# Rows of an expert stream sorted in fours, two blocks to a scatter, sixteen last slots

## The chip, the cores and the metric

The kernel runs on one core of a Trainium2 chip. Its time is device microseconds from launch to end, and lower is better. The kernel before takes 719.75 us (median of three runs, 718.98 to 726.15); the profiled execution has a span of 721.2 us and took 722.9 us.

Engines are named as in the profile: PE multiplies (PEld is its weight load), DVE works on vectors, ACT evaluates activations and copies, POOL here issues the indirect DMAs and zeroes a small tile, and SP issues the other DMAs. An indirect DMA is a scatter whose row addresses come from a tile.

## The reference

Eight sequences of 3584 tokens of 192 numbers go through a causal convolution of seven taps. Its taps are a softmax, one for each of eight groups of 24 channels. Then each of the 28,672 tokens goes to one of eight experts.

```python
logits = x @ w_gate                        # 28672 x 8, x is the convolution's result
e_idx = np.argmax(logits, axis=1)          # the token's expert
gate_w = probs[np.arange(N), e_idx]        # softmax of the logits
eom = 1.0 / (1.0 + np.exp(-(x @ w_output_gate)))
for e in range(E):
    mask = e_idx == e
    h = np.maximum(x[mask] @ w1[e], 0.0)   # 192 -> 1024
    ye = h @ w2[e]                         # 1024 -> 192
    out[mask] = gate_w[mask, None] * eom[mask, e, None] * ye
```

The inputs are drawn with a fixed seed. With them the experts get 3088, 3403, 4201, 3741, 3725, 3377, 3722 and 3415 tokens.

## The kernel before, in words

**Front.** The tokens come in 16 units of 1792. `front_a` (lines 356 to 424) convolves a unit with banded matrices (L367), transposes it (L390), multiplies it with the gates (L401) and transposes the logits back (L416). `front_b` (lines 427 to 550) picks each token's expert, counts, and sorts. A unit is sorted in eight steps of 224 tokens. In a step DVE makes two one-hot matrices `pm` of 120 x 256 (`prep`, L508) and gated rows `xrow` (L503). PE multiplies them in four products of 120 x 128 by 194 columns (L541). ACT copies the result into a tile `xs` (L548). The sorted rows of a step come as pairs: one partition of `xs` holds two rows of the same expert, so an expert's odd last row leaves a hole. One scatter (L559) writes the 128 partitions of `xs` to the DRAM stream `xcg`, where each expert has its own stretch. All counts and places (`R`, `DN`, `TP`, `CP`) are in pairs.

**Experts.** A slot is up to 512 rows of one expert's stretch. `slot_load` brings it in with two transposing DMAs, `xa` and `xb` (L682, L684), and the rows' token numbers `xi` (L686), all from SP. `Slot.first` multiplies with w1 (L727 with 128 rows of contraction, L734 with 64 rows, two at a time), and ACT and DVE apply the relu (L755, L753). `Slot.second` multiplies with w2 (L777). ACT copies 128 x 384 results to `y` (L783). Four scatters of 128 rows (L588) write a full slot's results to the output.

**Order.** The order is written out by hand. Before the main loop, units 0 to 3 are convolved and sorted. The main loop has iterations `u` = 2 to 13 of four slots each, and `u` = 14 with the last slots. A slot has four positions, so an iteration of four slots has positions 0 to 15. At each even position stands a `first` of half a slot, at each position a quarter of the `second` of the slot before. Around them the loop puts pieces of the front of later units. At positions 0 to 7 stand the eight sort steps of unit `u` + 2, one each, with the scatter of each right behind (`emit_in`). (In iteration 2 it is positions 3 to 10.) After position 7 SP gets the loads of the next iteration's slots. Output scatters are taken from a list by `quota`: one at each odd position among 0 to 7, then one and two in turn. `rest` puts a small POOL memset (L571) behind every second indirect DMA.

**Last slots.** `plan` chooses four experts for each iteration from 2 to 13 and takes up to 512 rows of each. For iteration 14, when all tokens are counted, it takes up to 512 rows of each of seven experts. Then `pick` chooses the expert with the most rows left, once for each entry of `DYN`: two slots of 512 rows and four of 256. For each, SP copies the expert's weights, 768 KB, to a tile `wd` (L704). What is still left goes through a loop at the end (L948), whose count is read from the rows left.

Of the kernel before, what the change touches and what calls it, by code (L numbers as in the profile page):

```python
# [11 lines left out]
FP16 = mybir.dt.float16  # L12
# [9 lines left out]
def kernel(  # L22
# [30 lines left out]
    TP = TT // 2  # L53
    NG = NB // 2
    CP = TP + N // 2 + 64
    CAP = 2 * CP
# [8 lines left out]
    DYN = (TP, TP) + (TP // 2,) * 4  # L65
# [5 lines left out]
    xcg2 = xcg.rearrange("(a b) w -> a (b w)", b=2)  # L71
# [153 lines left out]
    hole = const.tile([128, 1], FP32)  # L225
    nc.vector.tensor_scalar(out=rowi[:, 3:4], in0=rowi[:, 0:1], scalar1=63, scalar2=None,
                            op0=ALU.bitwise_and)
    nc.vector.tensor_copy(out=hole, in_=rowi[:, 3:4])
    nc.vector.tensor_scalar(out=hole, in0=hole, scalar1=float(HB), scalar2=-64.0,
# [22 lines left out]
    NXS = 12  # L252
    xss = [const.tile([128, 2, RW], FP16, name=f"xs{i}") for i in range(NXS)]
# [3 lines left out]
    poi = const.tile([128, 2, 128], U32)  # L257
    nc.gpsimd.iota(poi, pattern=[[1, 2], [2, 128]], base=1, channel_multiplier=0)
# [31 lines left out]
    for l in range(2):  # L290
        nc.vector.tensor_scalar(
            out=lsum[0:GE, l * GE:(l + 1) * GE].rearrange("p (i e) -> p i e", e=E),
            in0=s9[:, :, 0:E], scalar1=2.0, scalar2=None, op0=ALU.mult)
# [133 lines left out]
    def front_b(u, split=False):  # L427
# [30 lines left out]
        nc.vector.tensor_scalar(out=nu, in0=pn[:, 0:1], scalar1=1.0, scalar2=None,  # L458
                                op0=ALU.add)
        nc.vector.tensor_scalar(out=nu, in0=nu, scalar1=1, scalar2=None,  # L460
# [52 lines left out]
        if split:  # L513
# [10 lines left out]
            scalar=rowf[:, 0:1], in1=dd, op0=ALU.is_le, op1=ALU.mult)  # L524
        dst = pr.tile([128, NG], FP32, tag="dst", name="dst")
        nc.vector.tensor_reduce(out=dst, in_=dd, axis=AX.X, op=ALU.max)
        du = pr.tile([128, NG], U32, tag="du", name="du")
        nc.vector.tensor_scalar(out=du, in0=dst, scalar1=rowf[:, 0:1], scalar2=None, op0=ALU.add)
        prep(1)
        yield  # L530
        for i in range(NG):
            if i == 1 and u >= U0 and u != U0 + 2:
                v = u if u < U0 + 2 else u - 1
                plans[v] = plan(v)
            if i + 2 < NG:
                prep(i + 2)
# [7 lines left out]
            while len(pend) >= NXS:  # L544
                emit_in()
            xs = xss[nxs[0] % NXS]
            nxs[0] += 1
# [10 lines left out]
    def scatter(u, du, xs, i):  # L558
        i = nc.gpsimd.indirect_dma_start(  # L559
            out=xcg2, out_offset=bass.IndirectOffsetOnAxis(ap=du[:, i:i + 1], axis=0),  # L560
            in_=xs.rearrange("p r w -> p (r w)"), in_offset=None,
            bounds_check=E * CP - 1, oob_is_err=False)
        nodep(i, f"sc{u}", [f"sc{v}" for v in range(NU)] + ["load", "guard"])
# [40 lines left out]
    def plan_run(e0, n, nm):  # L604
# [8 lines left out]
        nc.vector.tensor_scalar(out=bu[:, 0:n], in0=bs, scalar1=2.0, scalar2=None, op0=ALU.mult)  # L613
        nc.vector.tensor_tensor(out=Dh, in0=Dh, in1=tk, op=ALU.add)
        nc.vector.tensor_scalar(out=tk, in0=tk, scalar1=-2.0, scalar2=float(TT),
# [15 lines left out]
    def plan(u):  # L631
        n = 4 if u < UL else E - 1
        e0 = nexte[0]
        nexte[0] = (e0 + n) % E
        p = plan_run(e0, min(n, E - e0), "a")
        if e0 + n > E:
            p += plan_run(0, e0 + n - E, "b")
        return p

    def pick(tp):  # L640
# [17 lines left out]
        nc.vector.scalar_tensor_tensor(out=bt, in0=bt, scalar=2.0, in1=oh,  # L658
# [9 lines left out]
        nc.vector.tensor_scalar(out=tk1, in0=tk1, scalar1=-2.0, scalar2=float(2 * tp),  # L668
# [39 lines left out]
    class Slot:  # L708
# [49 lines left out]
        def second(self, q):  # L758
# [15 lines left out]
            o = (q % 2) * D  # L774
            for fc in range(FCH):
                w = WA + (fc // 2 + fc % 2 * (FCH // 2)) * D
                nc.tensor.matmul(self.pp[:, o:o + D],  # L777
                                 self.ht[fc // 2][:, fc % 2, q * 128:(q + 1) * 128],
                                 self.w[:, w:w + D],
                                 start=(fc == 0 and q % 2 == 0),  # L780
                                 stop=(fc == FCH - 1 and q % 2 == 1))
            if q % 2 == 1:
                nc.scalar.copy(out=self.y[:, q - 1:q + 1, :],  # L783
                               in_=self.pp[:, 0:2 * D].rearrange("p (g d) -> p g d", d=D))
                pout.extend((self.y, self.oi, j) for j in (q - 1, q))
# [47 lines left out]
    def load_pick(tp):  # L833
        sel, bap, inv = pick(tp)
        base = reg(bap[0:1, 0:1], [ET.SP], E * CAP - TT)
        return w_dyn(sel), inv, slot_load(base, NU - 1, 2 * tp)
# [26 lines left out]
    for u in range(U0, UL + 1):  # L863
# [27 lines left out]
        while k < len(todo):  # L891
            w, inv, xabi = todo[k]
            s = Slot(xabi, w, inv)
            for q in range(4):
# [18 lines left out]
                if pos in sorting:  # L913
                    drain(fs, 1)
                    emit_in(len(pend))
# [22 lines left out]
    nc.vector.tensor_scalar(out=lfu, in0=lfu, scalar1=8, scalar2=None,  # L938
# [49 lines left out]
```

## Time and profile before

| | |
|---|---|
| time, median of 3 runs | 719.75 us |
| profiled execution, span | 722.9 us, 721.2 us |
| PE busy | 577.4 us (80%) |
| POOL busy | 419.3 us (58%) |
| DVE, ACT busy | 375.7 us, 364.8 us |
| stream scatters (L559) | 128, 128.9 us of POOL |
| output scatters (L588) | 236, 232.6 us of POOL |
| sort products (L541) | 512, 68.9 us of PE |
| first slot's first product, last iteration's first product | 100.3 us, 628.4 us |

So there are three stretches: the fill to 100.3 us, twelve iterations to 628.4 us (44.0 us each), and the last 13 slots to 721.2 us. The last two numbers of the table are the starts of L727 and L734 on the first and on the 49th slot. Read busy time by stretch, since the limits differ. The chain of waits follows the work that ended last back from the end. In it "another core or an unknown queue" is time in which the profile names no releaser; on one core this is no other core.

### The profile page before, as it was taken

How to read it: one execution, taken by the hardware profiler on the slowest of the kernel's cores; microseconds unless marked ns; L12 is line 12 of the kernel's file. 1: busy time of each engine (PE TensorE's matmuls, PEld its weight loads, DVE VectorE, ACT ScalarE, POOL GpSimd, SP SyncE). 2: the span in 40 equal slices, each digit the busy share in tenths (PEclk: the TensorE clock that was granted, in tenths of full speed). 3: DMA queues.
4: the chain of work that ended last, by engine and by line, in shares of the span. 5: the costliest groups of instructions: out<-in, count | busy, mean ns of one | idle time of the engine just before them, and what ended most of it. 6: DMA issues, size and time to landing. Idle time of an engine off the chain costs nothing.

```text
span 721.2 us, 16231 instructions
## 1 busy us (share of the span) xinstructions
PE 577.4 (80%) x5712; PEld 370.8 (51%) x5712; DVE 375.7 (52%) x1355; ACT 364.8 (51%) x657; POOL 419.3 (58%) x621
## 2 busy tenths in 40 slices
PE   8878868998497979869697897978969767688874
PEld 4545535664364646546364563644646434445552
DVE  6765547575344736546372673735638343146422
ACT  5765535664354635546363563644646444355552
POOL 8464443888455574655647355564655747555664
PEclk9976668999598998989899798997989989799998
DMA  9999493897555545355453544536142332576411
GB/s 166 235 265 225 105 190 78 165 197 149 112 126 115 126 118 129 93 131 129 108 126 109 102 124 103 135 100 130 69 101 71 88 80 74 118 161 199 156 55 36
DMA packets 161091, 91.95 MB, mean 127 GB/s; under 512 B 112373, under 2 KB 151910, under 8 KB 161008
## 3 DMA queue, kind: packets, MB, share of 16 engines
q1 hardware_dynamic: 131504, 47.57, 31.8%
q0 software_dynamic: 29504, 43.32, 22.7%
q8 instruction: 45, 0.74, 0.4%
q14 instruction: 38, 0.31, 0.2%
HBM read 37.87 MB, written 42.07 MB: 111 GB/s over the span
## 4 chain that ended last, share of the span: by engine, by line
PE 61%; another core or an unknown queue 10%; ACT 9%; issue 8%; DVE 5%; DMA 2%; POOL 2%; SPq 2%; POOLq 0%; ACTq 0%; DVEq 0%
PE pyt L777 18%; PE pp L727 16%; PE pp L734 8%; PE pf L541 6%; PE pf L367 6%; ACT ht L755 4%; PE pf L390 3%; PE pf L401 2%; DMA xt<-in_x_dram 1%; POOL out_dram L588 1%; ACT cv L349 1%; ACT tt L349 1%; ACT y L783 1%; DVE ht L753 1%
## 5 line engine op out<-in xcount | busy, mean ns | idle before, releaser
L588 POOL DMA_INDIRECT out_dram<-y,oi x236 | 232.6, 986 | 146.7 <-ACT y L783 82.3
L777 PE MATMUL pyt<-wres,ht 128*128 128x192 f16 x1760 | 188.3, 256 | 38.2 <-ACT y L783 20.9
L777 PEld LDWEIGHTS <-ht 128*128 128x128 f16 x1888 | 168.6, 101 | 82.6 <-issue 58.4
L559 POOL DMA_INDIRECT xcg_sorted<-xs,du x128 | 128.9, 1007 | 140.7 <-ACT xs L349 101.6
L755 ACT ACTIVATE ht<-pp 128x1024 f16<-128x1024 f32 (+1 forms) x183 | 176.5, 998 | 60.2 <-PE pp L727 30.1
L753 DVE TENSOR_SCALAR ht<-pp 128x1024 f16<-128x1024 f32 (+1 forms) x61 | 72.4, 1187 | 129.4 <-PE pp L727 92.4
L734 PE MATMUL pp<-xb,wres 64*128 64x512 f16 x220 | 75.6, 401 | 37.9 <-ACT ht L755 25.6
L783 ACT COPY y<-pyt 128x384 f32<-128x384 f32 x118 | 57.2, 484 | 94.6 <-remote 32.9
L727 PE MATMUL pp<-xa,wres 128*128 128x512 f16 x220 | 89.9, 409 | 1.3 <-issue 0.7
L727 PE MATMUL pp<-xb,wres 128*128 128x512 f16 x220 | 89.0, 404 | 2.2 <-issue 2.2
L367 PE MATMUL pf<-xt,band 64*64 64x192 f32 x1024 | 69.6, 368 | 20.9 <-issue 11.9
L349 ACT CAST xs<-pf 128x388 f16<-128x388 f32 x128 | 62.4, 496 | 43.1 <-PE pf L541 27.1
L734 PE MATMUL pp<-xa,wres 64*128 64x512 f16 x220 | 76.3, 404 | 1.3 <-issue 0.8
L541 PE MATMUL pf<-xrow,pm 120*128 120x194 f16 x512 | 68.9, 261 | 8.0 <-DVE pm L508 4.2
L351 DVE COPY cv<-pf 120x384 f32<-120x384 f32 x44 | 24.4, 556 | 96.5 <-remote 58.1
L727 PEld LDWEIGHTS <-wres 128*128 128x128 f16 x440 | 35.2, 101 | 64.1 <-issue 42.4
L349 ACT COPY cv<-pf 120x384 f32<-120x384 f32 x84 | 38.2, 486 | 55.1 <-remote 31.2
L508 DVE TENSOR_SCALAR pm<-pos,pos 120x256 f16<-120x256 f16 x256 | 61.5, 304 | 0.0
L503 DVE TENSOR_TENSOR xrow<-cv,gs 120x384 f16<-120x384 f32 x120 | 61.4, 550 | 0.0
L734 PEld LDWEIGHTS <-wres 64*128 64x128 f16 x440 | 18.4, 95 | 82.8 <-issue 82.1
L367 PEld LDWEIGHTS pf<-xt,band 64*64 64x64 f32 x1024 | 40.8, 146 | 36.9 <-issue 21.3
L541 PEld LDWEIGHTS <-pm 120*128 120x128 f16 x512 | 46.2, 102 | 16.9 <-DVE pm L508 6.5
(154 smaller groups left out, 526.0 us busy)
## 6 DMA issues: line engine op xcount, KB each, us to landing
xt<-in_x_dram SPq DMA_DIRECT2D x56, 384.0 KB
wd<-wres SPq DMA_DIRECT2D x6, 768.0 KB
out_dram<-y,oi POOLq DMA_INDIRECT x236
wres<-in_moe_w_dram POOLq DMA_DIRECT2D x8, 384.0 KB
xt<-in_x_dram SPq DMA_DIRECT2D x8, 336.0 KB
wres<-in_moe_w_dram POOLq DMA_DIRECT2D x8, 256.0 KB
xcg_sorted<-xs,du POOLq DMA_INDIRECT x128
xcg_sorted<-zrow SPq DMA_DIRECT2D x8, 256.0 KB
```

What stands on the lines that cost most here:

```text
L349: nc.scalar.copy(out=o, in_=i)
L367: nc.tensor.matmul(pcs[g][64 * c:64 * c + 64, o:o + NB // 2 * GH], band[64 * g:64 * g + 64, h + hh, :], xt[64 * g:64 * g + 64, c * NB // 2 ...
L508: nc.vector.tensor_scalar(out=pms[i][P, l, :], in0=pos16[P], scalar1=pos[P, l * NG + i:l * NG + i + 1], scalar2=None, op0=ALU.is_equal)
L541: nc.tensor.matmul(ps[:, r * XW:(r + 1) * XW], pm[P, l, r * 128:(r + 1) * 128], xr[P, l * NG + i, :], start=(r == 0 and l == 0), stop=(r = ...
L559: i = nc.gpsimd.indirect_dma_start(out=xcg2, out_offset=bass.IndirectOffsetOnAxis(ap=du[:, i:i + 1], axis=0), in_=xs.rearrange("p r w -> p ...
L588: i = nc.gpsimd.indirect_dma_start(out=out, out_offset=bass.IndirectOffsetOnAxis(ap=oi[:, j:j + 1], axis=0), in_=y[:, j, :], in_offset=Non ...
L727: nc.tensor.matmul(pps[r][:, l, :], w[:, o2:o2 + 128], x, start=(r == lead), stop=(r != lead))
L734: nc.tensor.matmul(pps[r][:, l, :], w[p0:p0 + 64, c:c + 128], x[p0:p0 + 64], start=(r != lead), stop=(r == lead))
L753: nc.vector.tensor_relu(out=ht, in_=pps[r])
L755: nc.scalar.activation(out=ht, in_=pps[r], func=AF.Relu)
L777: nc.tensor.matmul(self.pp[:, o:o + D], self.ht[fc // 2][:, fc % 2, q * 128:(q + 1) * 128], self.w[:, w:w + D], start=(fc == 0 and q % 2 = ...
L783: nc.scalar.copy(out=self.y[:, q - 1:q + 1, :], in_=self.pp[:, 0:2 * D].rearrange("p (g d) -> p g d", d=D))
```

## The change

A partition of `xs` now holds four rows of one expert (`QR` = 4), and all counts and places are in fours. A step's 224 tokens fill at most 64 such partitions, so two steps share one `xs` of 128 partitions and one scatter of 2 KB rows: four scatters a unit in place of eight. A step's one-hot matrix has the same 256 columns, read as four rows of 64. The products are 120 x 64 by 194 columns, and those of the two steps of a pair go side by side to columns 0 to 63 and 64 to 127 of PE. There are sixteen products for a pair of steps in place of eight. In the main loop both steps of a pair now stand at an odd position. The last iteration plans all eight experts, and `DYN` has eight entries: four slots of 512 rows, one of 256 and three of 128. Counted from the reference's routing, holes raise the stream's rows from 29,196 to 30,200, and with either kernel's last slots no row is left for the loop at the end.

```diff
-    TP = TT // 2
+    QR = 4
+    TP = TT // QR
...
-    CP = TP + N // 2 + 64
-    CAP = 2 * CP
+    NT = NG // 2
+    CP = TP + N // QR + 96
+    CAP = QR * CP
...
-    DYN = (TP, TP) + (TP // 2,) * 4
+    DYN = (TP,) * 4 + (TP // 2,) + (TP // 4,) * 3
...
-    NXS = 12
-    xss = [const.tile([128, 2, RW], FP16, name=f"xs{i}") for i in range(NXS)]
+    NXS = 6
+    xss = [const.tile([128, QR, RW], FP16, name=f"xs{i}") for i in range(NXS)]
...
-        du = pr.tile([128, NG], U32, tag="du", name="du")
-        nc.vector.tensor_scalar(out=du, in0=dst, scalar1=rowf[:, 0:1], scalar2=None, op0=ALU.add)
+        du = pr.tile([128, NT], U32, tag="du", name="du")
+        for g in range(2):
+            h = slice(64 * g, 64 * g + 64)
+            nc.vector.tensor_scalar(out=du[h], in0=dst[h].rearrange("p (t g) -> p g t", g=2)[:, g, :],
+                                    scalar1=rowm[h], scalar2=None, op0=ALU.add)
...
         for i in range(NG):
+            t, rh = i // 2, i % 2 * 2
...
-            pm = pms.pop(i)
             ps = pft()
             for r in range(2):
                 for l in range(2):
-                    nc.tensor.matmul(ps[:, r * XW:(r + 1) * XW],
-                                     pm[P, l, r * 128:(r + 1) * 128], xr[P, l * NG + i, :],
-                                     start=(r == 0 and l == 0), stop=(r == 1 and l == 1))
...
-            evac(xs[:, :, 0:XW], ps[:, 0:2 * XW].rearrange("p (r w) -> p r w", r=2), "act")
-            pend.append(lambda i=i, xs=xs: scatter(u, du, xs, i))
+                    for g in range(2):
+                        nc.tensor.matmul(
+                            ps[64 * g:64 * g + 64, r * XW:(r + 1) * XW],
+                            pms[2 * t + g][P, l, (rh + r) * 64:(rh + r + 1) * 64],
+                            xr[P, l * NG + 2 * t + g, :],
+                            start=(r == 0 and l == 0), stop=(r == 1 and l == 1),
+                            tile_position=(0, 64 * g))
...
+            evac(xs[:, rh:rh + 2, 0:XW], ps[:, 0:2 * XW].rearrange("p (r w) -> p r w", r=2), "act")
+            if rh:
+                pend.append(lambda t=t, xs=xs: scatter(u, du, xs, t))
...
-        n = 4 if u < UL else E - 1
+        n = 4 if u < UL else E
...
-                if pos in sorting:
-                    drain(fs, 1)
+                if pos in sorting and pos % 2:
+                    drain(fs, 2)
                     emit_in(len(pend))
```

PE, in the main loop, the end of a sort step before (`ht` is a slot's relu result, `pm` the one-hot matrix, `pf` the result in PSUM):

```order
L541 MATMUL pf_5411<-xrow1_249,pm_5320 128x194
L541 LDWEIGHTS pm_5320
L541 MATMUL pf_5411<-xrow1_249,pm_5320 128x194
L401 MATMUL pf_5423<-tt_5150,wg_128 32x224 x12
L734 LDWEIGHTS wres_307
```

and the middle of a pair of steps now, where the second half's result (`pf_5400`) begins:

```order
L549 LDWEIGHTS pm_5234
L549 MATMUL pf_5374<-xrow1_251,pm_5234 64x194
L549 LDWEIGHTS pm_5287
L549 MATMUL pf_5374<-xrow1_251,pm_5287 64x194
L549 LDWEIGHTS pm_5234
L549 MATMUL pf_5400<-xrow1_251,pm_5234 64x194
L549 LDWEIGHTS pm_5287
L549 MATMUL pf_5400<-xrow1_251,pm_5287 64x194
```

One step's `pm` fed four products in a row; now the `pm` of two steps alternate, product by product, through sixteen products.

POOL, in the main loop, from the sixth stream scatter of a unit to the outputs behind the last one, before:

```order
L559 DMA xcg_sorted<-xs_259,du 117248x512
L571 MEMSET idle 128x16
L559 DMA xcg_sorted<-xs_260,du 117248x512
L588 DMA out_dram<-y,oi 28672x192
L571 MEMSET idle 128x16
L559 DMA xcg_sorted<-xs_261,du 117248x512
L588 DMA out_dram<-y,oi 28672x192
L571 MEMSET idle 128x16
L588 DMA out_dram<-y,oi 28672x192 x2
```

and the last two stream scatters of a unit now:

```order
L572 DMA xcg_sorted<-xs_258,du 59136x1024
L601 DMA out_dram<-y,oi 28672x192
L584 MEMSET idle 128x16
L572 DMA xcg_sorted<-xs_259,du 59136x1024
L601 DMA out_dram<-y,oi 28672x192
L584 MEMSET idle 128x16
L601 DMA out_dram<-y,oi 28672x192 x2
```

Between two outputs there were one or two stream scatters and now there is one. Behind the last stream scatter of a unit stood twelve outputs up to the next unit's first; they stand there still, with a thirteenth, since the next unit's first stream scatter comes one position later.

## Rows read from the trace of the kernel before

**Rows 1.** The page: span, then busy time of each engine.
```profile
span 721.2 us, 16231 instructions
PE 577.4 (80%) x5712; PEld 370.8 (51%) x5712; DVE 375.7 (52%) x1355; ACT 364.8 (51%) x657; POOL 419.3 (58%) x621
```

**Rows 2.** Windows: stretch, length, busy time (count) of PE, PEld, DVE, ACT, POOL; clock.
```profile
367.20:387.60 20.40, 18.97 (x221) 13.57 (x222) 13.16 (x48) 12.53 (x22) 11.54 (x18) 1.00 0.48 122
387.60:413.10 25.50, 18.47 (x156) 10.73 (x153) 9.83 (x34) 9.90 (x17) 13.64 (x20) 0.80 0.48 104
628.40:690.60 62.20, 53.08 (x434) 31.89 (x433) 29.36 (x127) 34.21 (x45) 37.18 (x55) 1.00 0.58 159
690.60:721.20 30.60, 16.13 (x163) 11.25 (x160) 6.32 (x27) 9.80 (x19) 15.63 (x23) 0.91 0.13 44
```

**Rows 3.** Windows of line L727 alone (eight products a slot): PE busy (count), PEld.
```profile
100.30:628.40 528.10, 110.11 (x385) 31.17 (x386) 0.90 0.50 115
628.40:690.60 62.20, 21.58 (x72) 5.28 (x73) 1.00 0.58 159
```

**Rows 4.** Chain of waits, 374 to 386 us: start, length, what, count.
```profile
374.29 0.66 PE pyt L777 x8
374.95 0.34 PE pf L541 x4
...
381.38 1.72 PE pf L401 x24
...
385.27 0.22 PE pf L416 x2
```

**Rows 5.** Costliest groups: line, engine, names, shapes, count, busy us, mean ns, idle before.
```profile
L541 PE MATMUL pf<-xrow,pm 120*128 120x194 f16 x512 | 68.9, 261 | 8.0 <-DVE pm L508 4.2 <-issue 1.9 <-DVE xrow L503 1.4
L541 PEld LDWEIGHTS <-pm 120*128 120x128 f16 x512 | 46.2, 102 | 16.9 <-DVE pm L508 6.5 <-issue 6.4 <-DVE xrow L503 1.7
L367 PE MATMUL pf<-xt,band 64*64 64x192 f32 x1024 | 69.6, 368 | 20.9 <-issue 11.9 <-ACT cv L349 4.8 <-DVE gb L420 1.8
L559 POOL DMA_INDIRECT xcg_sorted<-xs,du x128 | 128.9, 1007 | 140.7 <-ACT xs L349 101.6 <-ACT tt L349 16.2 <-issue 15.9
L588 POOL DMA_INDIRECT out_dram<-y,oi x236 | 232.6, 986 | 146.7 <-ACT y L783 82.3 <-issue 45.7 <-DVE dd L522 4.9
```

**Rows 6.** POOL in order of time, 259 to 270 us: start, length, instruction, idle before.
```profile
259.59 0.97 POOL L559 DMA_INDIRECT xcg_sorted<-xs,du  x1 [1.75 <-ACT xs L349]
260.87 0.98 POOL L588 DMA_INDIRECT out_dram<-y,oi  x1 [0.30 <-issue]
...
268.58 0.99 POOL L588 DMA_INDIRECT out_dram<-y,oi  x1 [0.30 <-issue]
```

**Rows 7.** PE in order of time, 264 to 272 us.
```profile
264.25 0.87 PE L367 MATMUL pf<-xt,band 64*64 64x192 f32 x13
265.54 0.34 PE L367 MATMUL pf<-xt,band 64*64 64x192 f32 x1 [0.42 <-issue]
266.98 0.48 PE L367 MATMUL pf<-xt,band 64*64 64x192 f32 x2 [1.09 <-issue]
268.39 0.58 PE L734 MATMUL pp<-xb,wres 64*128 64x512 f16 x1 [0.94 <-issue]
...
271.26 0.60 PE L734 MATMUL pp<-xa,wres 64*128 64x512 f16 x1
```

**Rows 8.** The chain of waits, whole: shares by line, then two of its pieces.
```profile
by line: PE pyt L777 18.2%; PE pp L727 16.2%; another core or an unknown queue 10.4%; PE pp L734 8.5%; issue 7.9%; PE pf L541 5.7%; PE pf L367 5.7%; ACT ht L755 3.8%; PE pf L390 3.0%; PE pf L401 2.3%; DMA xt<-in_x_dram 1.2%; POOL out_dram L
...
94.19 4.05 another core or an unknown queue x2
...
388.83 7.99 another core or an unknown queue
```

**Rows 9.** POOL in order of time, 92 to 97 us, in the fill.
```profile
91.95 0.98 POOL L559 DMA_INDIRECT xcg_sorted<-xs,du  x1 [1.20 <-ACT xs L349]
...
95.80 0.98 POOL L559 DMA_INDIRECT xcg_sorted<-xs,du  x1 [0.31 <-issue]
```

More of the change, by code (lines that the diff above doesn't have):

```diff
@@ L225 @@
     hole = const.tile([128, 1], FP32)
+    rowm = const.tile([128, 1], FP32)
     nc.vector.tensor_scalar(out=rowi[:, 3:4], in0=rowi[:, 0:1], scalar1=63, scalar2=None,
@@ L228 @@
     nc.vector.tensor_copy(out=hole, in_=rowi[:, 3:4])
+    nc.vector.tensor_copy(out=rowm, in_=rowi[:, 3:4])
     nc.vector.tensor_scalar(out=hole, in0=hole, scalar1=float(HB), scalar2=-64.0,
@@ L251 @@
     nc.gpsimd.memset(lt, 0.0)
-    NXS = 12
-    xss = [const.tile([128, 2, RW], FP16, name=f"xs{i}") for i in range(NXS)]
+    NXS = 6
+    xss = [const.tile([128, QR, RW], FP16, name=f"xs{i}") for i in range(NXS)]
     for t in xss:
         nc.gpsimd.memset(t[:, :, XW:RW], 0.0)
-    poi = const.tile([128, 2, 128], U32)
-    nc.gpsimd.iota(poi, pattern=[[1, 2], [2, 128]], base=1, channel_multiplier=0)
+    poi = const.tile([128, QR, 64], U32)
+    nc.gpsimd.iota(poi, pattern=[[1, QR], [QR, 64]], base=1, channel_multiplier=0)
     pos16 = const.tile([128, 256], FP16)
@@ L457, in front_b @@
         nu = pr.tile([128, 1], U32, tag="nu", name="nu")
-        nc.vector.tensor_scalar(out=nu, in0=pn[:, 0:1], scalar1=1.0, scalar2=None,
+        nc.vector.tensor_scalar(out=nu, in0=pn[:, 0:1], scalar1=float(QR - 1), scalar2=None,
                                 op0=ALU.add)
-        nc.vector.tensor_scalar(out=nu, in0=nu, scalar1=1, scalar2=None,
+        nc.vector.tensor_scalar(out=nu, in0=nu, scalar1=2, scalar2=None,
                                 op0=ALU.logical_shift_right)
@@ L559, in scatter @@
         i = nc.gpsimd.indirect_dma_start(
-            out=xcg2, out_offset=bass.IndirectOffsetOnAxis(ap=du[:, i:i + 1], axis=0),
+            out=xcg4, out_offset=bass.IndirectOffsetOnAxis(ap=du[:, i:i + 1], axis=0),
             in_=xs.rearrange("p r w -> p (r w)"), in_offset=None,
@@ L657, in pick @@
                                        op0=ALU.add, op1=ALU.min)
-        nc.vector.scalar_tensor_tensor(out=bt, in0=bt, scalar=2.0, in1=oh,
+        nc.vector.scalar_tensor_tensor(out=bt, in0=bt, scalar=float(QR), in1=oh,
                                        op0=ALU.mult, op1=ALU.mult)
@@ L667, in pick @@
                                        op0=ALU.mult, op1=ALU.add)
-        nc.vector.tensor_scalar(out=tk1, in0=tk1, scalar1=-2.0, scalar2=float(2 * tp),
+        nc.vector.tensor_scalar(out=tk1, in0=tk1, scalar1=-float(QR), scalar2=float(QR * tp),
                                 op0=ALU.mult, op1=ALU.add)
@@ L774, in second @@
             o = (q % 2) * D
+            last = q % 2 == 1 or q == self.nq - 1
             for fc in range(FCH):
@@ L780, in second @@
                                  start=(fc == 0 and q % 2 == 0),
[L781 to L785, printed above, removed]
+                                 stop=(fc == FCH - 1 and last))
+            if last:
+                j0 = q - q % 2
+                nc.scalar.copy(out=self.y[:, j0:q + 1, :],
+                               in_=self.pp[:, 0:(q + 1 - j0) * D].rearrange("p (g d) -> p g d", d=D))
+                pout.extend((self.y, self.oi, j) for j in range(j0, q + 1))
     def reg(ap, engines, hi):
@@ L835, in load_pick @@
         base = reg(bap[0:1, 0:1], [ET.SP], E * CAP - TT)
-        return w_dyn(sel), inv, slot_load(base, NU - 1, 2 * tp)
+        return w_dyn(sel), inv, slot_load(base, NU - 1, QR * tp)
     xts[U0 + 3] = load_x(U0 + 3)
@@ L937 @@
     nc.vector.tensor_copy(out=lfu, in_=lf)
-    nc.vector.tensor_scalar(out=lfu, in0=lfu, scalar1=8, scalar2=None,
+    nc.vector.tensor_scalar(out=lfu, in0=lfu, scalar1=7, scalar2=None,
                             op0=ALU.logical_shift_right)
```

19 lines of the change are left out of this document (10 added, 9 removed).

## The prediction

> **What bounds the kernel now.** I read the busy times first. PE is busy 80% of the span and POOL 58%, so the scatters that the change halves are not on the engine with the most work [rows 1]. An average over the run hides the stretches, so I cut the main loop and the last slots into windows. In the first half of an iteration (367.2 to 387.6 us, with the sort steps) PE is busy 18.97 of 20.40 us. In the second half (387.6 to 413.1) it is busy 18.47 of 25.50: 7.0 us are lost there [rows 2]. The last slots are PE's as well: 53.08 of 62.20 us [rows 2].
>
> Where do the 7 us go? The chain of waits has 10.4% of the span, 75 us, without a releaser, in pieces like the 7.99 us at 388.83 [rows 8]. I looked at one of these with POOL beside PE. POOL waits for ACT's last `xs`, issues the last stream scatter at 259.59, and then seven output scatters without a pause until 269.57 [rows 6]. PE starts 13 products within 0.87 us at 264.25. From 265.54 on it starts one about every 1.4 us (265.54, 266.98, 268.39) and is still slow at 271.26 [rows 7]. So about 5 us into a run of back-to-back indirect DMAs PE slows, and it recovers 1 to 2 us after the run's end. The trace doesn't say why. It says that a long run costs PE time.
>
> **The change, part by part.** *Stream scatters.* 64 in place of 128 go, each 1.007 us of POOL [rows 5], and nine output scatters of 0.986 us come (245 in place of 236: 60 full slots of four, one half of two, three quarters of one). POOL gets 64.4 - 8.9 = 55.6 us less busy time. Most of this is worth nothing, since POOL idles 140.7 us ahead of these scatters, 101.6 of them for ACT's `xs` [rows 5]. If a scatter of 2 KB rows costs POOL twice as much, POOL is where it was, and no more.
>
> *Runs of scatters.* What could be worth something are the stalls of PE. The run that hurts begins with the last stream scatter of a unit, which waits for the last sort step in either kernel, and the seven outputs behind it were held back by `quota`, which is unchanged. In the order above the twelve outputs behind the last stream scatter stay as well. So this run keeps its eight scatters. Only where an earlier stream scatter was late too and joined the run does it become shorter. I take a tenth of the 75 us: **-7 us**. The bounds are 0 and the two scatters of 1.28 us (start to start in rows 6) that would leave each of twelve runs, -31 us.
>
> *Fill.* At 91.95 to 96.78 us four stream scatters run back to back [rows 9], and the chain has 4.05 us without a releaser at 94.19 [rows 8]. They become two. I take this piece as gone, **-4 us**. The bounds are 0 and -8, for a second such place. The rest of the fill keeps its convolutions and copies.
>
> *Sort products.* Four products now take 0.34 us [rows 4], so a pair of steps 0.68 us. In their place come 16 products of half the columns. Side by side without loss they take 0.68 us again. The nearest row is L401: 24 products of 224 columns in four column groups take 1.72 us on the chain, entry and exit included. L416 gives the rate of the same four-byte kind alone, 0.22 us for 2 x 128 columns or 0.86 ns a column [rows 4]. One after the other L401 would take 24 x 224 x 0.86 = 4.6 us, four at a time 1.16. So column groups do run side by side here, with 0.56 us of loss for 24 products, 0.37 for 16. L367, in groups of rows and columns, has 69.6 us for 64 blocks of 16 [rows 5], 1.09 each against 0.66. I take 0.25 us a pair, less than these two, as the loads are two-byte ones and the groups two. In the main loop there are 48 pairs, in the half of the iteration where PE has 1.4 us to spare, so all of it counts: **+12 us**. The 16 pairs in the fill I cost at nothing: PE waits there for other things, and without that cover they add 4 us. The lower bound is 0. The upper bound is a load of 0.102 us [rows 5] ahead of every product with nothing beside it: 16 x 0.102 = 1.63 us, 0.95 more a pair, +46 us. The Trainium skill, TensorEngine Tiling (Array Packing), under Restrictions and Gotchas, says that column tiling excludes the fast weight load, and under Key Properties that changing the tiling mode drains the engine. By that rule the sum would tend to this upper bound; the 1.72 us of L401 speak against it, as they hold loads and a change of mode too.
>
> *What moves with them.* A scatter leaves one step later for even steps and at the same step for the last, so the loads that SP holds until the last scatter of a unit has landed start when they did. ACT copies the same 128 results, two behind each other. They wait behind `y` now, which no longer stands between two of them. One more DVE instruction a unit writes `du`. Both engines are about 60% busy there (13.16 and 12.53 of 20.40 us) [rows 2]: nothing, and if `xs` came late, the next transposes would wait for a PSUM tile, a few tenths a pair, within the bound above.
>
> *Last slots.* The holes raise the stream from 29,196 to 30,200 rows. The slots' room grows from 59 x 512 to 61.25 x 512 rows, and slots are computed in full, however few rows they hold. 72 products of L727 at eight a slot are nine full slots in 62.20 us [rows 2, 3], 6.91 us each. Now there are twelve (eight planned, four picked): +20.7 us. Behind them stand one half and three quarter slots in place of four halves. The 30.60 us of these and the end hold 16.13 us of PE [rows 2], some 4 a slot. A quarter has half of a half's columns and results, at most 2 us less; I take 1.7, three times: -5.1. Sum **+15.6 us**. The bounds: +20.7 if a quarter costs what a half did, since its weights' copy is as large. Below, three full slots at PE's own 53.08 / 9 = 5.90 us, and the quarters at half of 30.60 / 4: 17.7 - 11.5 = +6.2. Two more copies of 768 KB run eight slots ahead of their use, and the DMA engines are 58% busy there (the last but one number in rows 2).
>
> The sum is 15.6 + 12 - 7 - 4 = **+16.6 us**. It is made against the profiled execution (722.9 us, 721.2 of them span: 739.5). That one lies 3.2 us above the median of the runs shown, so I add the difference to the median: 719.75 + 16.6 = **736 us**. The likeliest case has 727 to 752 as its own range.
>
> **Rivals.** *The runs get shorter (faster).* If PE is slowed not by the run alone but by all the indirect DMAs of the 10 us before it, half the stream scatters take two off each run: -31 us. With sort products at 0 and the fill at -8 it is 15.6 - 31 - 8 = -23, 697 us. It decides the case from about 2.5 us of PE's loss an iteration on. For it: each lost stretch stands beside a run. Against it: the run's first scatter waits for ACT, so those before are done. 0.15.
>
> *Nothing moves.* The sort costs 0, the last slots 11, and the runs and the fill give back 11: 720 us. For it: L367's and L401's groups do overlap. Against it: PE has little room in the first half of an iteration. 0.22.
>
> *The products don't run side by side.* At +46 for the sort the sum is 15.6 + 46 - 11 = +51, 770 us. This is what the skill's page on tiling would lead to. L401 speaks against it. It decides from 0.5 us a pair on. 0.13.
>
> *The slots don't hold the rows.* Then the loop at the end would run, a whole slot with no overlap each time. Counted from the reference's routing, no row is left. 0.02.
>
> The forecast has 0.48.
>
> **How the numbers follow.** About 1% (7 us) is what can be told from no change here. Faster is the first rival, 0.15. The same is the second, 0.22. Slower is the forecast and the two others: 0.63. The range leaves out most of the first rival and the upper half of the third, about 0.2: **711 to 764 us**.
>
> **What would show it.** Twelve full slots of about 6.9 us behind the 49th slot, and a main loop that begins at about 96 us. On PE a pair of sort steps as one block of 0.8 to 1.0 us; 0.7 would make the sort free, 1.5 would be the third rival. In the second half of an iteration still one scatter and seven outputs back to back, with 6 to 7 us lost; if the run has five outputs or PE loses under 4 us, the first rival is right. The time without a releaser in the chain should be near 65 us. I am wrong if the last slots take under 100 us, or if the main loop is more than 10 us shorter than 528.

## The result, and the profile after

The changed kernel takes 697.63 us (median of four runs, 692.4 to 697.9) beside 719.37 us for the kernel before: ratio 0.9669, interval 0.9602 to 0.9736. It is faster, where 736 us had been forecast. (For e1, e2 and e8 below, the median leaves out one run in a slower state.)

That holds on one kind of chip. The experiments ran on five chips. On one of them, called A here, the kernel before took 717 to 720 us (medians); the result's own chip is not on record, but its times are A's. On the four others, called B, it took 555.8 to 557.3 us. Runs on A stand before and after those on B (e1 to e4, then e17 and e18), so the difference goes with the chip and not with the time of day. The change was run again on one chip of B and is slower there: 576.67 beside 556.38 us, ratio 1.0374, interval 1.0295 to 1.0454 (e9). The forecast's sum was +16.6 us; A measured -21.7, B +20.3. So the document has two questions: where A's gain is from, and which steps of the forecast hold on B.

The page of the changed kernel on A, the rows that answer to [rows 1]:

```profile
span 695.8 us, 17364 instructions
PE 585.8 (84%) x6344; PEld 373.4 (54%) x6344; DVE 388.0 (56%) x1414; ACT 377.4 (54%) x672; POOL 362.1 (52%) x532
```

PE has 8 us more work, POOL 57 less. Three windows each, for the fill, the main loop and the last slots (from the starts of the first and the 49th slot's first product); columns as in [rows 2]. The kernel before:

```profile
0.00:100.30 100.30, 78.04 (x907) 48.65 (x908) 61.88 (x268) 57.39 (x150) 58.59 (x107) 0.82 0.90 196
100.30:628.40 528.10, 430.15 (x4218) 279.05 (x4216) 278.16 (x935) 263.40 (x443) 307.87 (x438) 0.90 0.50 115
628.40:721.20 92.80, 69.20 (x594) 43.14 (x592) 35.68 (x153) 44.01 (x64) 52.80 (x77) 0.97 0.43 122
```

The changed kernel:

```profile
0.00:89.80 89.80, 71.39 (x1034) 46.36 (x1034) 63.32 (x273) 57.36 (x150) 37.62 (x74) 0.92 0.95 206
89.80:580.70 490.90, 427.14 (x4601) 272.39 (x4599) 280.89 (x947) 266.96 (x443) 262.67 (x370) 0.91 0.59 127
580.70:695.80 115.10, 87.23 (x715) 54.66 (x712) 43.79 (x195) 53.04 (x79) 61.85 (x90) 0.91 0.45 120
```

The fill is 10.5 us shorter, the main loop 37.2, and the last slots are 22.3 us longer: -25.4, the difference of the spans. These are single profiles, and on A they repeat less well than the whole time: where the kernel before's code is the same, its fill takes 95.9 to 100.3 us (e1, e2, e17), its main loop 518.1 (e1) or 528.1, its last slots 92.8 to 98.6 (e2, e17). So the first and the last difference are uncertain by some 5 us, the middle one by 10. In the main loop PE is busy as long as before (427 and 430 us), with more instructions. What went is idle time of PE, from 98 to 64 us.

The chain of waits of the changed kernel says the same of the main loop. "Another core or an unknown queue" was 10.4% in [rows 8] and is about 1% now:

```profile
PE 69%; issue 7%; ACT 4%; DVE 3%; DMA 1%; another core or an unknown queue 1%; POOL 0%; ACTq 0%
```

This chain can be followed back only to 91 us, so it says nothing of the fill. The stall that [rows 6, 7] show is still there once an iteration. POOL in order of time, the last stream scatter of a unit (L572) and the outputs behind it (L601):

```profile
194.19 0.98 POOL L572 DMA_INDIRECT xcg_sorted<-xs,du  x1 [2.37 <-ACT xs L353]
195.47 0.98 POOL L601 DMA_INDIRECT out_dram<-y,oi  x1 [0.30 <-issue]
...
203.18 0.98 POOL L601 DMA_INDIRECT out_dram<-y,oi  x1 [0.30 <-issue]
```

PE in order of time beside it:

```profile
201.40 0.24 PE L791 MATMUL pyt<-wres,ht 128*128 128x192 f16 x1
202.11 0.24 PE L791 MATMUL pyt<-wres,ht 128*128 128x192 f16 x1 [0.47 <-issue]
202.96 0.24 PE L791 MATMUL pyt<-wres,ht 128*128 128x192 f16 x1 [0.61 <-issue]
204.35 0.24 PE L791 MATMUL pyt<-wres,ht 128*128 128x192 f16 x1 [1.15 <-issue]
205.33 0.32 PE L791 MATMUL pyt<-wres,ht 128*128 128x192 f16 x1 [0.73 <-issue]
```

One scatter and seven outputs back to back, and from about 7 us into them PE starts one product in 0.7 to 1.4 us, with nothing to wait for ("issue"). That this run would stay is what the forecast had said.

In the fill it is otherwise. Where the kernel before had four stream scatters back to back [rows 9], POOL's last four are now apart:

```profile
82.07 1.00 POOL L572 DMA_INDIRECT xcg_sorted<-xs,du  x1 [7.42 <-ACT xs L353]
84.38 0.98 POOL L572 DMA_INDIRECT xcg_sorted<-xs,du  x1 [1.31 <-ACT xs L353]
...
88.67 0.98 POOL L572 DMA_INDIRECT xcg_sorted<-xs,du  x1 [1.11 <-ACT ex L441]
```

PE waited there for ACT's copy of a convolution (`cv`) ahead of its last products of the fill. Before and now:

```profile
98.81 1.55 PE L367 MATMUL pf<-xt,band 64*64 64x192 f32 x14 [4.23 <-ACT cv L349]
```

```profile
89.02 0.88 PE L371 MATMUL pf<-xt,band 64*64 64x192 f32 x14 [0.37 <-ACT cv L353]
```

In e1, e2 and e17, whose fill is that of the kernel before, PE is idle for 2.2 to 4.5 us ahead of the same products.

The costliest groups that answer to [rows 5], the scatter of two blocks, the sort products and their weight loads:

```profile
L572 POOL DMA_INDIRECT xcg_sorted<-xs,du x64 | 64.2, 1003 | 142.4 <-ACT xs L353 121.2
...
L549 PE MATMUL pf<-xrow,pm 120*64 120x194 f16 x1024 | 63.9, 260 | 16.0 <-DVE pm L512 14.0
...
L549 PEld LDWEIGHTS <-pm 120*64 120x64 f16 x1024 | 44.9, 113 | 30.9 <-DVE pm L512 17.9
```

A scatter of 2 KB rows costs POOL what one of 1 KB did, and 1024 products of 64 columns keep PE busy no longer than 512 of 128 did.

### The profile page after: what moved, and what is told of

Its sections match the earlier page's. It is cut to its first block, busy times and chain, and to the rows that moved or that the text cites. A ratio compares the mean times of both kernels' runs of the same rounds, so it can differ in the third digit from the quotient of the medians.

```text
span 695.8 us, 17364 instructions
## 1 busy us (share of the span) xinstructions
PE 585.8 (84%) x6344; PEld 373.4 (54%) x6344; DVE 388.0 (56%) x1414; ACT 377.4 (54%) x672; POOL 362.1 (52%) x532
## 3 DMA queue, kind: packets, MB, share of 16 engines
q0 software_dynamic: 28912, 43.83, 25.7%
## 4 chain that ended last, share of the span: by engine, by line
PE 69%; issue 7%; ACT 4%; DVE 3%; DMA 1%; another core or an unknown queue 1%; POOL 0%; ACTq 0%
PE pyt L791 24%; PE pp L740 19%; PE pp L747 9%; PE pf L371 6%; PE pf L549 5%; PE pf L394 3%; PE pf L405 2%; ACT y L798 2%; ACT ht L768 1%; DMA wres<-in_moe_w_dram 1%; DVE ht L766 1%; ACT xs L353 1%; DVE pm L512 0%; DVE xrow L507 0%
## 5 line engine op out<-in xcount | busy, mean ns | idle before, releaser
L601 POOL DMA_INDIRECT out_dram<-y,oi x245 | 243.5, 994 | 169.7 <-ACT y L798 105.9
L791 PEld LDWEIGHTS <-ht 128*128 128x128 f16 x1960 | 174.6, 101 | 98.5 <-issue 74.3
L768 ACT ACTIVATE ht<-pp 128x1024 f16<-128x1024 f32 (+2 forms) x192 | 183.2, 987 | 53.5 <-PE pp L740 36.2
L766 DVE TENSOR_SCALAR ht<-pp 128x1024 f16<-128x1024 f32 (+2 forms) x64 | 75.3, 1177 | 114.9 <-PE pp L740 92.1
L572 POOL DMA_INDIRECT xcg_sorted<-xs,du x64 | 64.2, 1003 | 142.4 <-ACT xs L353 121.2
L798 ACT COPY y<-pyt 128x384 f32<-128x384 f32 (+1 forms) x124 | 58.9, 475 | 109.7 <-PE pp L740 40.9
L549 PE MATMUL pf<-xrow,pm 120*64 120x194 f16 x1024 | 63.9, 260 | 16.0 <-DVE pm L512 14.0
L353 ACT CAST xs<-pf 128x388 f16<-128x388 f32 x128 | 57.3, 495 | 17.1 <-PE pf L549 16.0
L549 PEld LDWEIGHTS <-pm 120*64 120x64 f16 x1024 | 44.9, 113 | 30.9 <-DVE pm L512 17.9
L353 ACT COPY tt<-pf 128x448 f32<-128x448 f32 x63 | 32.0, 545 | 23.6 <-PE pf L394 14.6
```

The lines of the kernel that those rows point to most:

```text
L353: nc.scalar.copy(out=o, in_=i)
L549: nc.tensor.matmul(ps[64 * g:64 * g + 64, r * XW:(r + 1) * XW], pms[2 * t + g][P, l, (rh + r) * 64:(rh + r + 1) * 64], xr[P, l * NG + 2 * ...
L572: i = nc.gpsimd.indirect_dma_start(out=xcg4, out_offset=bass.IndirectOffsetOnAxis(ap=du[:, i:i + 1], axis=0), in_=xs.rearrange("p r w -> p ...
L601: i = nc.gpsimd.indirect_dma_start(out=out, out_offset=bass.IndirectOffsetOnAxis(ap=oi[:, j:j + 1], axis=0), in_=y[:, j, :], in_offset=Non ...
L766: nc.vector.tensor_relu(out=ht, in_=pps[r])
L768: nc.scalar.activation(out=ht, in_=pps[r], func=AF.Relu)
```

## The experiments on chip A

**The change's last slots alone (e1).** In the kernel before, with an odd last quarter copied by itself as in the change:

```diff
-    DYN = (TP, TP) + (TP // 2,) * 4
+    DYN = (TP,) * 4 + (TP // 2,) + (TP // 4,) * 3
-        n = 4 if u < UL else E - 1
+        n = 4 if u < UL else E
```

> The kernel before with the change's last slots alone (eight planned, eight picked; rows still sorted in pairs). By the two profiles the stretch from the 49th slot on grew from 92.8 to 115.1 us: this kernel should then be 20 to 24 us slower than before, 741 us, its main loop within 3 us of 528. If the prediction's term (+15.6) was right and the rest of the growth belongs to the rows in fours, 735 us.

736.03 beside 719.92 us, ratio 1.0238 [1.0171, 1.0305]: 16 us more (17 by the ratio), between the two expectations. In its profile the last stretch is 112.8 us, 20.0 more than before. Its main loop, whose code is that of the kernel before, takes 518.1 us where I had expected 528 within 3. So these slots are a loss, and the gain in the other two stretches is larger than the 22 us of the result.

**The order alone (e2).** In the kernel before:

```diff
-                if pos in sorting:
-                    drain(fs, 1)
+                if pos in sorting and pos % 2:
+                    drain(fs, 2)
```

> The kernel before with the change's places for the sort steps alone: both steps of a pair, and both of their scatters, at the odd position; eight scatters a unit as before. Theory 'fewer scatters' (the 37 us of the main loop come from POOL issuing half the stream scatters): main loop within 8 us of 528, time 712 to 727. Rival 'order' (they come from the steps standing together at odd positions): main loop near 491, time near 683.

730.54 us, ratio 1.0132 [1.0087, 1.0177]; its main loop has 538.0 us. Slower by 11 us (1.3%), outside both expectations: the new places are no gain, and with eight scatters a unit they may cost.

**The scatters cut in two (e3).** In the changed kernel, with `du2` twice `du` and one more:

```diff
-                pend.append(lambda t=t, xs=xs: scatter(u, du, xs, t))
+                for h in range(2):
+                    pend.append(lambda t=t, xs=xs, h=h: scatter(u, du2, xs, t, h))
...
-            in_=xs.rearrange("p r w -> p (r w)"), in_offset=None,
+            in_=xs[:, 2 * h:2 * h + 2, :].rearrange("p r w -> p (r w)"), in_offset=None,
```

> The changed kernel with each stream scatter cut into two of 1 KB rows (the first two and the last two rows of each four): again 128 stream scatters, with the sort products, the order and the last slots of the change. 'Fewer scatters': the main loop goes back by 20 to 37 us and the fill by 5 to 10, time 723 to 745. 'Order', or the products' new form: 698 within 4 us.

755.93 us, ratio to before 1.0472 [1.0407, 1.0536]: 58 us above the change, more than the highest expectation. Its three windows:

```profile
0.00:109.60 109.60, 85.24 (x1036) 53.71 (x1036) 63.97 (x281) 57.83 (x150) 56.12 (x101) 0.80 0.83 179
109.60:640.90 531.30, 433.56 (x4601) 279.93 (x4599) 283.01 (x971) 266.65 (x443) 309.76 (x440) 0.90 0.51 115
640.90:753.20 112.30, 87.09 (x715) 53.48 (x712) 44.65 (x195) 53.70 (x79) 61.32 (x89) 0.93 0.44 124
```

Both gains are gone: the main loop has 40.4 us more than the change's, the fill 19.8. The sort products, the order, the rows and the last slots are the change's, and so are the bytes that the scatters move. Their queue in the page of e3, where the change has 28912 packets and 43.83 MB:

```profile
q0 software_dynamic: 29936, 43.84, 22.8%
```

So on A the gain is the 64 stream scatters that POOL no longer issues, 60.2 / 64 = 0.94 us each on average; e3 does not tell their number from the longer runs that they make.

**The outputs spread evenly (e4).** In the changed kernel:

```diff
-            if pos in sorting:
-                return pos % 2
-            return 1 + pos % 2
+            return 1
```

> The changed kernel with quota 1 at every position of the main loop: the output scatters spread evenly, so that fewer of them stand back to back behind the last stream scatter of a unit. If a long run of back-to-back indirect DMAs is what slows PE there (some 6 us an iteration left), the main loop becomes 25 to 60 us shorter: 640 to 673 us. If PE slows there for another reason (SP's loads of the next slots, which start when that last scatter has landed), it stays at 698 within 7.

664.47 us, ratio to before 0.9194 [0.9134, 0.9253], 33 us below the change, with the same number of indirect DMAs. Its main loop:

```profile
89.50:548.90 459.40, 411.52 (x4601) 269.61 (x4599) 283.42 (x947) 263.32 (x443) 259.40 (x370) 0.97 0.64 134
```

PE is idle for 48 us of it in place of 64, and the same 4601 products take 411.5 us in place of 427.1, at a granted clock of 0.97 in place of 0.91. (1.00 is the upper of the clock's two levels, 2.4 GHz; the lower, 1.2 GHz, is 0.50.) In the change the stretch right behind the stall that is shown above has PE busy again, at 0.60:

```profile
206.00:213.00 7.00, 6.95 (x51) 3.96 (x55) 5.08 (x19) 4.35 (x8) 2.09 (x3) 0.60 0.47 93
```

So idle time of PE is paid twice here: as such, and by a lower clock for the work behind it. e4's second expectation is out: the loads of the next slots, which the edit leaves as they are, are not by themselves what slows PE.

**The same for the kernel before (e17).** Quota 1 at every position of iterations 4 to 12:

> The kernel of e15, for a chip where PE slows: 675 to 695 us if the length of the runs sets what PE loses (nine iterations without their run of eight or more), 720 within 7 if only the number of indirect DMAs does. Where PE does not slow: the same as before, as in e15.

727.17 beside 717.46 us, ratio 1.0166 [1.0086, 1.0246]: a little slower, far from the first expectation and just above the second. In its profile the main loop takes 527.5 us, as before, and the last slots 98.6. With eight scatters a unit, two scatters and two outputs meet in every two positions of the sort, and they stick together.

A count from the traces of A shows it. A run is a row of indirect DMAs less than 0.6 us apart; beside each I counted the time in which PE neither multiplied nor loaded weights, from its start to 1.7 us after its end, in the main loop (number of runs x mean idle us):

| kernel on A | runs of 3 | of 4 | of 5 to 7 | of 8 to 13 | idle beside all runs |
|---|---|---|---|---|---|
| before | 22 x 0.46 | 2 x 2.51 | 7 x 1.02 | 10 x 5.93 | 83.6 |
| change | 1 x 0.60 | 1 x 0.00 | 1 x 3.02 | 10 x 4.28 | 53.0 |
| e3, scatters in two | 29 x 0.63 | 1 x 1.83 | 10 x 3.48 | 3 x 7.59 | 84.9 |
| e4, change, even | 33 x 0.37 | 3 x 1.46 | 4 x 1.86 | none | 34.5 |
| e17, before, even | 5 x 0.95 | 19 x 1.09 | 7 x 2.42 | 7 x 4.90 | 81.0 |

(The column of all runs holds those of one and two as well. The stretches counted are 84 to 90% of the main loop, so that most of the idle time lies beside a run tells nothing; how it differs with the length of the run does.) Runs of three cost about half a microsecond and runs of eight or more 4 to 8. The even quota in e17 turns runs of three into runs of four and five, and its sum stays at 81 us; with half the scatters gone (e4) the runs are of three and none is longer than seven. So the length of the runs goes with the loss, and the number of scatters sets how short runs can be. That is what the table bears out. Length alone is not all of it: a run of five to seven lost 1.02 us in the kernel before and 3.48 in e3.

**The sort products by column group (e18).** In the changed kernel `for g` becomes the outermost of the three loops.

> The changed kernel with the eight sort products of a step ordered by column group: four to columns 0 to 63, then four to columns 64 to 127, where the change alternates between the groups. Where PE does not slow, a block of 16 products takes 0.79 us now. If alternating is what lets two groups run side by side, the products follow each other at 0.085 us each (0.34 us for four in the kernel before): 16 take 1.36 us, 0.57 more for each of 48 pairs, 27 us slower than the change (604 us). If the order makes no difference, 577 us. Where PE slows, 27 us or nothing beside the change's 698 us.

696.99 us, the same as the change. On the chain a block of 16 products, the change and then e18:

```profile
178.73 0.79 PE pf L549 x16
```

```profile
186.98 0.81 PE pf L549 x16
```

The alternation of the two groups is not what makes them cheap. A product of 64 columns takes 0.050 us in either order, one of 128 columns 0.085 (0.34 for four in [rows 4]). What sets the 0.050 is open.

## The experiments on chips B

**The change itself (e9).**

> The changed kernel itself, beside the kernel before on one chip. On the chip of the runs e1 to e4 the kernel before took 720 us and PE slowed beside every run of indirect DMAs; on the chip of e5 to e8 it took 556 us and PE did not slow. Theory 'the gain is the slowing': on a chip of the second kind the change has nothing to win and pays for its last slots and its holes, 15 to 25 us slower than before (571 to 581 us); on a chip of the first kind it is 20 to 25 us faster again. Rival 'fewer scatters are worth something everywhere': faster than before on either.

576.67 beside 556.38 us, ratio 1.0374 [1.0295, 1.0454]: slower, as the first theory says.

**The kernel before itself (e11), and with the change's last slots (e12, the edit of e1).**

> The kernel before itself, for its profile on a chip where PE does not slow (556 us). Theory 'the terms were right there': its last slots take 14 to 16 us less than the 93.7 us of the changed kernel in e9, an iteration at its steady rate 0.7 to 1.0 us less than 32.5 (four pairs of sort steps at 0.17 to 0.25 us), its fill about 4 us less than 87.7. On a chip where PE slows it repeats 720 us.

> The kernel of e1 (before, with the change's last slots alone) for the other kind of chip. Where PE does not slow: 14 to 17 us slower than before (nine full slots of 5.65 become twelve, 17.0, less 1 to 3 for three quarters in place of halves), so these slots are most of the change's 20 us there. Where PE slows: 18 us slower, as in e1.

e11 repeats 557 us. e12 takes 570.03 beside 556.86 us, ratio 1.0214 [1.0167, 1.026]: +13.2 us, just under what was expected. Windows of the kernel before on B (e11):

```profile
0.00:83.80 83.80, 67.92 (x906) 42.17 (x906) 62.08 (x268) 56.62 (x150) 53.76 (x100) 0.94 0.96 215
83.80:474.10 390.30, 377.81 (x4217) 259.51 (x4214) 278.48 (x938) 267.19 (x444) 312.33 (x435) 0.99 0.72 157
474.10:554.40 80.30, 66.83 (x592) 42.68 (x592) 34.96 (x149) 44.78 (x63) 59.79 (x87) 0.94 0.64 158
```

and of the change on B (e9), with one steady iteration as a fourth row:

```profile
0.00:87.70 87.70, 70.62 (x1035) 46.44 (x1036) 62.72 (x273) 57.12 (x150) 37.96 (x74) 0.92 0.97 210
87.70:479.20 391.50, 384.50 (x4602) 260.42 (x4600) 280.67 (x948) 265.99 (x443) 259.66 (x365) 0.99 0.74 157
479.20:572.90 93.70, 79.62 (x714) 50.62 (x711) 44.57 (x195) 54.54 (x79) 65.51 (x95) 0.94 0.60 159
228.50:261.00 32.50, 32.50 (x401) 22.27 (x400) 23.89 (x84) 22.63 (x38) 21.24 (x31) 1.00 0.67 156
```

On B PE is busy 378 of the main loop's 390 us. There is little to win, and each stretch of the change is longer: +3.9, +1.2, +13.4 (e9 and e11 ran on two chips of B; the kernel before has the same time on both within 0.1%). The steady iteration is 32.53 us between the slots' first products; that of the kernel before is 31.76, with PE as full:

```profile
226.40:258.20 31.80, 31.80 (x371) 22.12 (x371) 23.81 (x83) 22.67 (x38) 26.04 (x37) 1.00 0.66 159
```

**Longer runs on B (e6, and the same kernel in e14 and e16).** In the changed kernel `quota` is 0 at the sorting positions and 2 at the others.

> The changed kernel with quota 0 at the sorting positions and 2 at the others: the same output scatters, held back into one longer run. If the length of the run sets what PE loses, 20 to 60 us slower than the change: 718 to 758 us. If only their number counts, 698 within 7.

> The kernel of e6, for a chip where PE slows: 718 to 758 us if the length of the run sets what PE loses, 698 within 7 if only the number of indirect DMAs does. Where PE does not slow: 4% slower than before once more, like the change itself.

> The kernel of e6, for a chip where PE slows: 718 to 758 us if the length of the run sets what PE loses, 698 within 7 if only the number of indirect DMAs does. Where PE does not slow: 580 us, as in e6 and e14.

579.46, 580.11 and 580.77 us on three chips of B, 3 to 4 us above the change in e9. In e14 a scatter and sixteen outputs stand back to back from 216.06 us on. The kernel before goes further: in e11 173 indirect DMAs follow each other less than 0.6 us apart from 150.2 to 378.3 us. Windows of e14 and of e11 there (PE's one wait ahead of 160 us is one for a slot's rows, shown below):

```profile
216.00:238.90 22.90, 22.90 (x273) 15.48 (x268) 18.84 (x65) 16.08 (x27) 18.77 (x27) 1.00 0.61 140
```

```profile
160.00:379.00 219.00, 218.80 (x2512) 152.08 (x2512) 159.72 (x543) 153.78 (x259) 178.77 (x249) 0.99 0.71 163
```

Beside the eight of the change on A, for comparison:

```profile
199.60:206.00 6.40, 2.15 (x16) 1.17 (x14) 0.00 (x0) 0.48 (x1) 3.89 (x6) 0.90 0.60 138
```

On B PE loses nothing in 22.9 us of scatters and 0.2 us in 219, on A 4.25 us in 6.4. Since these three experiments ran on B, the longer run was not measured on A.

**The kernel before with even outputs (e5, again as e10 and e13; in the middle iterations alone, e15).**

> The kernel before with quota 1 at every position of the main loop, nothing else. If runs are what costs PE time, they go here too: main loop 30 to 55 us shorter, 665 to 690 us. If half the stream scatters are worth something beyond shorter runs (37 us), it lands near 684 (664 of the changed kernel with even outputs, less 18 for the last slots, plus 37). If the change's gain was nothing but shorter runs, it lands near 646 to 655.

> The kernel before with quota 1 at every position once more, for a chip of the first kind. There, if runs of scatters are what costs PE time, the main loop is 30 to 55 us shorter and the time 665 to 690 us; near 684 if half the stream scatters are worth 37 us beyond that. On a chip of the second kind, 1% slower than before, as in e5.

> The kernel of e5, for a chip where PE slows: 665 to 690 us if the length of runs is what costs PE time, near 684 if half the stream scatters are worth 37 us beyond that. Where PE does not slow: 1% slower than before once more.

> The kernel before (pairs, its own last slots) with quota 1 at every position of iterations 4 to 12 alone; the first two iterations and the last keep the old quota. In e13 the even quota cost its 1% only there (11.9 to 12.5 us in place of 8.1 to 10.7 for slots 6 and 7, and 3.5 us at slots 47 and 48), while the steady iteration was 31.77 us with either. So where PE does not slow: 556 to 558 us, the same as before. Where PE slows: nine iterations lose their run of eight or more scatters and save 3 to 5 us each, 675 to 695 us.

On B 562.59, 562.31 and 563.17 us, ratios 1.010 to 1.012: 1% slower, which says nothing on A. In the middle iterations alone it is 557.73 beside 557.27 us, the same as before; e17 shows that it is no gain on A either.

**Fitted slots (e7) and later loads (e8).** e7 is e4 with `DYN = (TP,) + (TP * 3 // 4,) * 4 + (TP // 4,) * 2`; in e8 the changed kernel issues `loads` at position 11.

> Even outputs (quota 1) and picked slots cut to the rows that are left: one of 512 rows, four of 384, two of 128 in place of four of 512, one of 256, three of 128. If a slot costs by its columns, 384 rows and one small slot fewer are 5 + 3 us: 656 us. If a slot of 384 costs what one of 512 does (its weights' copy and its wait are the same), 661 us.

> The changed kernel with SP's loads of the next slots issued at position 11 instead of 7, so that their transposing DMAs no longer lie beside the run of eight scatters. If the run alone slows PE, the loss of about 6 us an iteration beside it stays, and the time is 690 to 712 us (a wait for later loads may come). If run and transposes are both needed, PE no longer slows there: 650 to 680 us.

e7 takes 573.23 beside 555.79 us, ratio 1.0303 [1.0267, 1.0339], some 3 us below e9's 576.67 on another chip of B. Its last slots take 89.3 us in place of 93.7 and its main loop 391.5 as in e9. So the fitted slots give 4.4 us, where 8 or 3 were expected, and the even outputs give nothing on B. e8 takes 589.57 us, ratio 1.0614 [1.0548, 1.068], 13 above e9: loads issued later cost. Whether they would free PE on A was not measured. Of all kernels run, e4 is the fastest on A; on B none beats the kernel before.

## Why the prediction was wrong

| us | forecast | A | B |
|---|---|---|---|
| last slots | +15.6 | +22.3 | +13.4 |
| sort products, main loop | +12 | +9.2, from B | +9.2 |
| runs: the main loop without these | -7 | -46.4 | -8.0 |
| fill | -4 | -10.5 | +3.9 |
| sum | +16.6 | -25.4 | +18.5 |

**The step that failed** is the one on runs, "I take a tenth of the 75 us: -7", with its bound of -31, and ahead of it "most of this is worth nothing, since POOL idles 140.7 us ahead of these scatters". POOL's time was taken as free because POOL is not the bound. On A it isn't free: e3 prices a stream scatter at 0.94 us of the whole kernel's time, nearly the 1.007 us that it takes on POOL in [rows 5]. I had looked only at the run that is longest in every iteration. That run did stay at eight and loses what it did: 3.4 to 5.4 us in the kernel before where it has eight, 3.7 to 5.1 in the change. What went were the runs of 3 to 7 (31 of them with 22 us of idle became 3 with 4 us) and the four of ten to thirteen, with 6 to 10 us of idle each: by these, mean idle beside the ten runs of 8 to 13 fell from 5.93 to 4.28 us, 16.5 us in all. A sign that I had named for being wrong came with it: a main loop of 490.9 us, more than 10 below 528. And 1% of the chain is without a releaser, where I had 65 us. The bound counted two scatters at the end of twelve runs, not what each scatter costs PE wherever it stands.

**The first rival** had the time (697 us) and half the mechanism: all the indirect DMAs around count. That its sum met the time is partly luck: it had the sort products at 0, the last slots at +15.6 and the runs at -31. Its sign, a run of five or less than 4 us lost, did not come; nor did the forecast's 6 to 7 us, since the runs of eight lost 4.28 us on average. Its chance of 0.15 was too low. What I held against it, that the run's first scatter waits for ACT and those before it are done, is true of the long run alone; beside the 22 runs of three PE lost 10 us as well, and I had not looked there.

**Sort products.** The blocks of 0.8 to 1.0 us came, at 0.79. At B's steady rate the change costs 32.53 - 31.76 = 0.77 us an iteration, 0.19 a pair of steps: 9.2 us in twelve iterations, where I had 0.25 a pair and 12. The third rival and its upper bound are out. The Trainium skill, TensorEngine Tiling (Array Packing), under Restrictions and Gotchas, has column tiling without the fast weight load. The trace fits that as far as it goes: a load of 64 columns took 113 ns, one of 128 columns 102 [rows 5]. But at 0.050 us a product, load included, no price of it shows in the block. [rows 4]'s L401 was the better guide.

**Fill.** On B it is 3.9 us longer, about the 4 us that I named as the price "without that cover". On A it is 10.5 us shorter, and the 16 scatters that e3 puts back there cost 19.8 us: the same failed step once more. I had priced one piece of 4 us, which went (4.23 to 0.37 us), and a possible second.

**Last slots.** Twelve full slots came, at 6.87 us each (82.40 us for twelve), as forecast. What stands behind them is mis-sized. The change on A:

```profile
580.70:663.10 82.40, 72.38 (x580) 43.44 (x578) 38.99 (x172) 45.34 (x60) 49.38 (x72) 0.98 0.60 159
663.10:695.80 32.70, 14.86 (x138) 11.22 (x135) 4.81 (x24) 7.70 (x19) 12.47 (x18) 0.75 0.07 23
```

One half, three quarters and the end take 32.7 us in place of the 30.60 in [rows 2]; I had -5.1 for them, and +2.1 came. PE has 1.3 us less work there, but at a granted clock of 0.75 in place of 0.91. On B a full slot takes 5.65 us in the change; twelve take 67.8 and the rest 25.9 (e9), beside 51.7 for nine and 28.6 (e11): +16.1 and -2.7. My lower price for three slots, 17.7 from PE's own time, was the right kind there.

So on B the sum lies within 2 us of the forecast, but this is partly luck. The last slots and the sort products came within 3 us. The fill has the other sign, and the -8.0 is not the forecast's term, since PE does not slow beside scatters there: it is what remains of +1.2 when the 9.2 of twelve steady iterations are taken off. Part of it are two waits for a slot's rows in the main loop of e11, which e9 does not have:

```profile
PE pp L734 <- DMA xb<-xcg_sorted: 4.0, 1, 4.0
PE pp L727 <- DMA xa<-xcg_sorted: 2.4, 1, 2.4
```

On A one term is wrong by 39 us, and it decides the sign of the whole.

## What to carry to other kernels

Time of an engine that is not the bound is free only if the bound engine runs on undisturbed beside it: where a trace shows one engine slowed beside another's work, price each instruction that goes away at its full length, wherever it stands, and let that be the bound. On a chip like A, long runs of scatters are worth breaking up (e4), but only where there is room between them (e17). And time a change on more than one chip: here one edit is 3% faster on one and 4% slower on another.

## What the runs showed of the hardware

**The chips differ.** The same program, 719.9 us on A and 555.8 to 557.3 on four others. Of the main loop's difference of 138 us, 85 lie in PE's idle time (528.10 - 430.15 = 98 beside 390.30 - 377.81 = 12) and 52 in the same products at a granted clock of 0.90 beside 0.99; the clocks' ratio alone makes 38 of these (378 x 0.99 / 0.90 = 416). The engines' own work is alike: an output scatter takes POOL 994 ns on A and 1001 on B in the change, and the transfers of the scatters and the instructions take the same time, in the pages of the change on A

```profile
q0 software_dynamic: 28912, 43.83, 25.7%
q8 instruction: 50, 0.82, 0.5%
```

and on B (e9):

```profile
q0 software_dynamic: 28912, 43.83, 31.4%
q8 instruction: 50, 0.82, 0.6%
```

(shares of 16 engines' span: 2861 and 2878 us of engine time for the scatters, some 55 for the instructions on either). The Trainium skill, Runtime: NRT & Kernel Launch, under Instruction fetch mechanics, has a sequencer fetch blocks of 16 KiB through a queue of its own, mostly hidden. The 50 packets of 0.82 MB have that size, and their transfers are not slower on A; whether they are hidden no run shows. Why PE starts its instructions so slowly beside scatters on A, no run shows.
